# Top-k attention feeding a SwiGLU block: gate and value products of the first four token blocks by halves, and another order of the small units

## The chip, the cores and the metric

The kernel runs on one core of one Trainium2 chip. The metric is the time of one execution on the device in microseconds; lower is better. A profile of one execution stands beside the times.

## What is computed

For 8 batches of 8 heads, with 576 tokens and 64 dimensions a head, scores are q·k divided by 8. Each row keeps its scores down to the 32nd largest; the others become -1e9, and a softmax over the row weighs the values. The heads' results side by side give 4608 tokens of 512 numbers, which pass a SwiGLU block:

```python
scores = scale * np.matmul(q, k.transpose(0, 1, 3, 2))
kth = np.partition(scores, -top_k, axis=-1)[..., -top_k:-top_k + 1]
scores = np.where(scores >= kth, scores, -1000000000.0)
...
x = np.ascontiguousarray(attn_out.transpose(0, 2, 1, 3)).reshape(B * S, H * D)
g = x @ w_gate
silu = g * (1.0 / (1.0 + np.exp(-g)))
return (silu * (x @ w_val) @ w_out).astype(np.float32)
```

w_gate and w_val are 512 x 1536, w_out is 1536 x 512. All is float32.

## The kernel before, in words

**Attention units.** The work of attention is cut into 160 units (`units`). A whole unit is 128 queries of a pair of heads; a batch has 4 such query tiles for each of its 4 pairs. The 64 queries that are left in a batch make a small unit for each pair, in which both heads share the 128 partitions: it has half the work on DVE. A unit passes these steps, each a function: `scores` (PE matmuls L341, for a small unit L327, ACT copies to `sc`), `select` (DVE: four rounds of MAX8 L362, with three rounds of MATCH_REPLACE8 L366 between them, then L372, which writes the penalty into `e`), `penalize` (POOL: L382 and L384, `e` += `sc`), `weigh` (ACT: exp L393), `normalize` (DVE reciprocal L405, ACT L408), `turn` (PE transposes L420, ACT copies L421) and `values` (PE L440 and L449, ACT copy L460 into `xT`).

**FFN blocks.** `xT[kb]` holds a block of 256 tokens (BLK), all 4 pairs of heads; there are 18 blocks, and `done[kb]` counts the columns that have been written. `feed(kb)` is a generator of a block's FFN work: for each of 6 steps s a gate product and a value product, each 8 matmuls of 256 moving columns (L499) into one tile of a PSUM pool with three buffers (`ps_f`). After a product, ACT works on the tile (for the gate L524 to L526, for the value L531) and POOL multiplies (L527, L532). Then comes the product with `w_out`: block 0 has 24 matmuls of 512 columns (L545, `plain`), every other block seven quarters of 6 matmuls (L585) with sums on POOL (L592, L600, L605, L633 and L571).

**Weights.** The generator `weights` brings the three matrices in 36 pieces and rounds them in three steps: a DMA into `w` (three buffers), three ACT instructions (L116, L118, L119), then a DVE shift (L123) and two POOL instructions (L124, L125). The numbers in `lags` say how many half steps after its start a piece takes its last, second and first step. `ready[0]` counts finished pieces. `need(n)` pushes the generator on until n pieces are ready.

**Order.** Nothing is left to a scheduler: at the end, each engine's instructions are tied to the order in which the program issued them. The main loop goes over n. In round n it issues `penalize(n-1)`, `turn(n-3)`, `values(n-4)`, `scores(n+1)`, `weigh(n-1)`, `select(n)` and `normalize(n-2)`, and in between calls `pieces(k)`, which issues up to k pieces of FFN work, and `rounding(1)` (five times in a round with a whole unit). A piece is 4 matmuls of a product, or 3 of a quarter. `credit` limits the pieces: `share(n)` adds 6.4 or 7 for a whole unit, less what the attention of that round takes on PE, and at most one more than that is kept from round to round. `piece` starts a new block when the block before it is finished and `done` says that all 256 columns are there; else it returns 0. It also flushes the queues `on_act` and `on_pool`, in which the ACT and POOL work on products waits, when two are in them. After the last round, all that is left of the FFN work is issued.

**Small units.** Even batches have their small units last, odd ones first. The loop after `units` mixes, for each even batch, its 4 small units, those of the next batch and the first 4 whole units of the next batch: two small ones, a whole one, and so on.

Of the kernel before, what the change touches and what calls it, by code (L numbers as in the profile page):

```python
# [8 lines left out]
AF = mybir.ActivationFunctionType  # L9
ALU = mybir.AluOpType  # L10
FP32 = mybir.dt.float32
# [4 lines left out]
P = 128  # L16
# [4 lines left out]
BLK = 256  # L21
# [4 lines left out]
def kernel(  # L26
# [39 lines left out]
    nc = tc.nc  # L66
    B, H, S, D = q.shape
    DM, DFF = w_gate.shape
    J = S // P
    JP = J * P  # L70
    R = S - JP
    NHP = H // 2
    KC = DM // P
    MC = DFF // P
    MS = MC // 2
    MQ = MC // 2
    NBLK = B * S // BLK
    scale = 1.0 / float(D) ** 0.5
# [8 lines left out]
    ffn = ctx.enter_context(tc.tile_pool(name="ffn", bufs=2))  # L87
# [13 lines left out]
    wg = consts.tile([P, KC, DFF], FP32, name="wg")  # L101
    wv = consts.tile([P, KC, DFF], FP32, name="wv")
# [24 lines left out]
    def weights():  # L127


        pieces = []  # L130
        for f in range(0, DFF, WP):
            for src, dst in ((w_gate, wg), (w_val, wv)):
                for c in range(0, KC, 2):
                    rows = src[c * P : (c + 2) * P, f : f + WP]
                    pieces.append((
                        rows.rearrange("(c p) f -> p c f", p=P), dst[:, c : c + 2, f : f + WP]
                    ))
        for c in range(MC):
            pieces.append((
                w_out[c * P : (c + 1) * P].rearrange("p (c f) -> p c f", c=2),  # L140
                wo[:, c].rearrange("p (c f) -> p c f", c=2),
            ))
        pieces = [rounded(*p) for p in pieces]
        step = [0] * len(pieces)

        def upto(i, k):

            while 0 <= i < len(pieces) and step[i] < k:
                next(pieces[i], None)
                step[i] += 1  # L150


        lags = (3, 2, 0)
        for n in range(2 * len(pieces) + 4):
            for k, lag in enumerate(lags):
                if (n - lag) % 2 == 0:
                    upto((n - lag) // 2, len(lags) - k)
            ready[0] = max((n - 5) // 2 + 1, 0)
            early[0] = lambda: upto(n // 2, 2)
            yield  # L160
        early[0] = lambda: None


        add, sub = ALU.add, ALU.subtract
        lo, hi = slice(0, DM // 2), slice(DM // 2, DM)
        room = []
        for _ in range(3):
            t = ffn.tile([P, 4, DM // 2], FP32, tag="w", name="t", bufs=3)
            room += [t[:, 0:2], t[:, 2:4]]
        for m in range(0, MQ, 2):  # L170
            mm, nn = slice(m, m + 2), slice(MQ + m, MQ + m + 2)
            t3 = room.pop()
            nc.gpsimd.tensor_tensor(t3, wo[:, nn, hi], wo[:, mm, hi], sub)
            T[7] += [t3[:, i, :] for i in range(2)]
            yield
        while not plain_done:
            yield
        for m in range(0, MQ, 2):
            mm, nn = slice(m, m + 2), slice(MQ + m, MQ + m + 2)
            t1 = wo[:, mm, hi]  # L180
            nc.gpsimd.tensor_tensor(t1, t1, wo[:, mm, lo], sub)
            T[5] += [wo[:, m + i, hi] for i in range(2)]
            yield
            t2 = room.pop()
            nc.gpsimd.tensor_tensor(t2, wo[:, nn, hi], t1, sub)
            T[6] += [t2[:, i, :] for i in range(2)]
            yield
            t4 = conv.tile([P, 2, DM // 2], FP32, tag="size", name="t4", bufs=3)
            nc.gpsimd.tensor_tensor(t4[:], wo[:, nn, lo], t2, sub)
            T[4] += [t4[:, i, :] for i in range(2)]  # L190
            yield
        T[1] += [wo[:, m, lo] for m in range(MQ)]
        T[2] += [wo[:, MQ + m, lo] for m in range(MQ)]
        T[3] += [wo[:, MQ + m, hi] for m in range(MQ)]
        yield
# [5 lines left out]
    weight = weights()  # L201
# [2 lines left out]
        for _ in range(n):  # L204
            next(weight, None)

    def need(n):

        while ready[0] < n:
            next(weight)  # L210

    pairs = [(b, hp) for b in range(B) for hp in range(NHP)]
    raw, preps = {}, {}
# [62 lines left out]
    def column(b, qt):  # L276

        return b * S + (qt * P if b % 2 == 0 else 0 if qt == J else R + qt * P)
# [1 line left out]
    units = [(b, qt, hp) for b in range(B) for qt in tiles(b) for hp in range(NHP)]  # L280


    for b in range(0, B - 1, 2):
        n0 = (b * (J + 1) + J) * NHP
        mixed = units[n0 : n0 + 3 * NHP]
        small_ends, small_begins, whole = (
            mixed[i * NHP : (i + 1) * NHP] for i in range(3)
        )
        small_ones = [
            small_ends[0], small_ends[1], small_ends[2], small_begins[0],  # L290
            small_ends[3], small_begins[1], small_begins[2], small_begins[3],
        ]
        units[n0 : n0 + 3 * NHP] = [
            x for i in range(NHP) for x in (*small_ones[2 * i : 2 * i + 2], whole[i])
        ]
    same_pair = {}
    for n, (b, _, hp) in enumerate(units):
        same_pair.setdefault((b, hp), []).append(n)
# [182 lines left out]
    def flush(queue):  # L481
        while queue:
            queue.pop(0)()

    def feed(kb):

        x = xT.pop(kb)  # L490
        hs = []

        def product(w, s, then):
            ps = ps_f.tile([P, 2, BLK], FP32, tag="f", name="f")
            need(4 * s + (2 if w is wg else 4))
            for i in range(2):
                m = 2 * s + i
                for kc in range(KC):
                    nc.tensor.matmul(  # L499
                        ps[:, i, :],  # L500
                        w[:, kc, m * P : (m + 1) * P],
                        x[:, kc, :],
                        start=(kc == 0),
                        stop=(kc == KC - 1),
                    )
                if i == 1:
                    on_act.append(lambda: then(ps))
                yield 1

        plain = kb == 0  # L510
        first, late = slice(0, P), slice(P, BLK)
# [2 lines left out]
            "p (m t) -> p m t", t=P  # L514
        )

        for s in range(MS):
            h = ffn.tile([P, 2, BLK], FP32, tag="h", name="h", bufs=MS + 1)
            hs.append(h)


            def gate(ps, h=h):
                half = ffn.tile([P, 2, BLK], FP32, tag="gv", name="half_g", bufs=3)
                nc.scalar.activation(h[:], ps[:], AF.Tanh, scale=0.5)  # L524
                nc.scalar.mul(half[:], ps[:], 0.5)
                nc.scalar.add(h[:], h[:], 1.0)  # L526
                on_pool.append(lambda: nc.gpsimd.tensor_mul(h[:], h[:], half[:]))  # L527

            def value(ps, h=h, s=s):
                val = ffn.tile([P, 2, BLK], FP32, tag="gv", name="val", bufs=3)  # L530
                nc.scalar.copy(val[:], ps[:])  # L531
                on_pool.append(lambda: nc.gpsimd.tensor_mul(h[:], h[:], val[:]))  # L532

            yield from product(wg, s, gate)
            yield from product(wv, s, value)
        o = ffn.tile([P, 2, DM], FP32, tag="o", name="o", bufs=1)
        if plain:
            for t in range(2):
                ps = ps_f.tile([P, DM], FP32, tag="f", name="o_ps")
                for m in range(MC):  # L540
                    need(4 * MS + m + 1)
                    if m == 6:
                        flush(on_act)
                        flush(on_pool)
                    nc.tensor.matmul(  # L545
                        ps[:],
                        hs[m // 2][:, m % 2, t * P : (t + 1) * P],
                        wo[:, m, :],
                        start=(m == 0),
                        stop=(m == MC - 1),  # L550
                    )
                    if m == MC - 1:

                        def finish(ps=ps, t=t):
                            nc.scalar.copy(o[:, t, :], ps[:])
                            store(o[:, t, :], kb * BLK + t * P)

                        on_act.append(finish)
                        if t == 1:
                            plain_done.append(True)  # L560
                    if m % 2 == 1:
                        yield 1
            return
# [123 lines left out]
    current = []  # L687

    def piece():

        if len(on_act) > 1:
            flush(on_act)
        if len(on_pool) > 1:
            flush(on_pool)
        while True:
            if not current:
                if not todo or done.get(todo[0], 0) < NHP * BLK:
                    return 0
                flush(on_act)
                flush(on_pool)  # L700
                current.append(feed(todo.pop(0)))
            cost = next(current[0], 0)
            if cost == 0:
                current.pop()
                continue
            return cost

    def fetch(n):

# [18 lines left out]
        return beside * n_heads(units[n][1]) / 2 - others  # L728

    def pieces(n):  # L730
        for _ in range(n):
            if credit[0] >= 1:
                credit[0] -= piece()

    def run(steps):
        for _ in steps:
# [128 lines left out]
```

## Time and profile before

| | us |
|---|---|
| median of 8 runs (1825.26 to 1828.7) | 1825.59 |
| the profiled execution | 1827.02 |
| its span, first to last instruction | 1825.2 |
| PE busy / weight loads | 1701.4 / 1404.4 |
| DVE busy | 1612.9 |
| ACT busy | 1218.1 |
| POOL busy | 1040.7 |

The profile comes from the hardware's profiler. "Busy" is the time in which an engine had at least one instruction; PE's matmuls overlap, so their mean duration (383 ns for 256 columns) is longer than the distance between them. A float32 matmul leaves two records in the trace, a transpose one. "Granted clock" is the share of PE's full clock. The slices of the profile cut the span into 40 parts of 45.6 us, each with a digit for tenths of busy time. In a list by time, each line merges instructions of one group: start, duration, group and count, and in brackets the idle time before it and what ended it.

### The profile page before, as it was taken

The page shows a single profiled execution, that of the slowest core. Times are in us where ns is not written, and L with a number is a line of the kernel's source. Part 1 is how long each engine was busy: PE and PEld are TensorE (multiplying, and loading weights), DVE is VectorE, ACT ScalarE, POOL GpSimd, SP SyncE. Part 2 cuts the span into 40 slices and gives each one's busy share as a digit, 9 for nine tenths or more (in the row PEclk, how much of TensorE's full clock was granted, in tenths as well). Part 3 has the DMA queues.
Part 4 walks back from the last instruction along what each step waited for, and adds up shares of the span by engine and source line. Part 5 has one row for each costly group of instructions (what it writes and reads, how often), then busy time and mean ns, then how long its engine had stood idle before and what let it go on. Part 6 is the DMA issues. An engine that isn't in the chain of part 4 may idle for free.

```text
span 1825.2 us, 30457 instructions
## 1 busy us (share of the span) xinstructions
PE 1701.4 (93%) x10756; PEld 1404.4 (77%) x10756; DVE 1612.9 (88%) x3372; ACT 1218.1 (67%) x2945; POOL 1040.7 (57%) x930
## 2 busy tenths in 40 slices
PE   3458999999999999799999999999999999999999
PEld 2346767788888877688888867788888878788888
DVE  7999999999999898999999988999999989998500
ACT  6788767676767576667767676667776767575532
POOL 5878654656464645466565635474556554555544
PEclk6768999999999999899999999999999999999999
DMA  7433011001200011001200011000200011000000
GB/s 195 130 95 103 15 40 42 14 1 39 52 13 1 13 42 41 14 1 31 60 13 1 12 43 41 15 8 7 71 19 7 7 23 40 7 12 1 13 12 12
DMA packets 109033, 59.65 MB, mean 33 GB/s; under 512 B 88272, under 2 KB 96720, under 8 KB 108880
## 3 DMA queue, kind: packets, MB, share of 16 engines
q1 hardware_dynamic: 107680, 57.30, 11.7%
q8 instruction: 85, 1.39, 0.3%
q14 instruction: 68, 0.56, 0.1%
q10 hardware_dynamic: 1200, 0.39, 0.1%
HBM read 48.23 MB, written 9.44 MB: 32 GB/s over the span
## 4 chain that ended last, share of the span: by engine, by line
PE 84%; DVE 6%; ACT 5%; POOL 3%; issue 2%; DMA 0%; SPq 0%; POOLq 0%; DVEq 0%; ACTq 0%
PE f L499 42%; PE x_ps L585 8%; PE av L449 8%; PE etps L420 8%; PE s L341 7%; PE y_ps L585 6%; DVE m L362 2%; DVE rest L366 2%; PE s L327 1%; PE av L440 1%; ACT e L393 1%; PE o_ps L545 1%; PE kqps L265 1%; POOL e L384 1%; ACT e L408 1%
## 5 line engine op out<-in xcount | busy, mean ns | idle before, releaser
L362 DVE MAX8 m<-rest 128x8 f32<-128x576 f32 x864 | 616.7, 753 | 2.2
L366 DVE MATCH_REPLACE8 rest<-m,rest 128x576 f32<-128x576 f32 x576 | 425.7, 749 | 0.0
L384 POOL TENSOR_TENSOR e<-e,sc 128x1152 f32<-128x1152 f32 (+1 forms) x160 | 383.0, 2394 | 71.6 <-DVE e L372 59.4
L499 PE MATMUL f<-xT,wg 128*128 128x256 f32 x1728 | 402.9, 383 | 0.0
L499 PE MATMUL f<-xT,wv 128*128 128x256 f32 x1728 | 399.8, 382 | 0.0
L499 PEld LDWEIGHTS f<-xT,wg 128*128 128x128 f32 x1728 | 322.7, 190 | 65.4 <-issue 23.5
L499 PEld LDWEIGHTS f<-xT,wv 128*128 128x128 f32 x1728 | 323.9, 190 | 58.5 <-issue 16.2
L527 POOL TENSOR_TENSOR h<-h,half_g 128x512 f32<-128x512 f32 x108 | 139.8, 1294 | 338.4 <-ACT h L526 331.9
L421 ACT COPY et<-etps 128x512 f32<-128x512 f32 (+2 forms) x448 | 184.3, 484 | 156.8 <-PE etps L420 155.8
L362 DVE MAX8 m<-sc 128x8 f32<-128x576 f32 x288 | 205.9, 753 | 85.4 <-ACT sc L346 50.5
L420 PE MATMUL etps<-ident,e 128*128 128x128 f32 (+1 forms) x1312 | 185.2, 285 | 98.3 <-issue 37.0
L393 ACT ACTIVATE e<-e,bias 128x576 f32<-128x576 f32 x288 | 221.7, 774 | 80.7 <-POOL e L384 80.6
L420 PEld LDWEIGHTS etps<-ident,e 128*128 128x128 f32 (+1 forms) x1312 | 158.1, 146 | 128.5 <-issue 45.3
L532 POOL TENSOR_TENSOR h<-h,val 128x512 f32<-128x512 f32 x108 | 142.0, 1315 | 163.2 <-ACT val L531 163.0
L408 ACT ACTIVATE e<-e,tot 128x576 f32<-128x576 f32 x288 | 211.7, 790 | 1.9 <-DVE tot L405 1.8
L366 DVE MATCH_REPLACE8 rest<-m,sc 128x576 f32<-128x576 f32 x288 | 212.5, 747 | 0.0
L372 DVE TENSOR_SCALAR e<-sc,m 128x576 f32<-128x576 f32 x288 | 184.2, 680 | 3.4
L341 PE MATMUL s<-kqT 64*128 64x288 f32 x1024 | 171.3, 451 | 8.9 <-ACT kqT L270 8.9
L449 PE MATMUL av<-et,v 128*64 128x128 f32 (+1 forms) x2560 | 170.1, 278 | 0.0
L346 ACT COPY sc<-s 128x288 f32<-128x288 f32 x512 | 164.5, 403 | 3.1 <-PE s L341 3.1
L449 PEld LDWEIGHTS av<-et,v 128*64 128x64 f32 x2560 | 133.7, 142 | 22.6 <-issue 5.9
L524 ACT ACTIVATE h<-f 128x512 f32<-128x512 f32 x108 | 65.3, 605 | 127.6 <-PE f L499 127.6
(73 smaller groups left out, 2028.9 us busy)
## 6 DMA issues: line engine op xcount, KB each, us to landing
v<-in_v_dram SPq DMA_DIRECT2D x32, 256.0 KB, 2.9
kq_in<-in_k_dram SPq DMA_DIRECT2D x63, 128.0 KB, 2.9
kq_in<-in_q_dram SPq DMA_DIRECT2D x63, 128.0 KB, 2.9
out_dram<-o SPq DMA_DIRECT2D x31, 256.0 KB, 2.4
w<-in_moe_w_gate_dram SPq DMA_DIRECT2D x12, 512.0 KB, 3.7
w<-in_moe_w_val_dram SPq DMA_DIRECT2D x12, 512.0 KB, 3.8
w<-in_moe_w_out_dram SPq DMA_DIRECT2D x12, 512.0 KB, 3.6
out_dram<-o SPq DMA_DIRECT2D x9, 128.0 KB, 2.3
```

Of the source, the lines that this page charges most:

```text
L341: nc.tensor.matmul(ps[:, 0:half], slab[d, q0 : q0 + P], slab[d, k0 : k0 + half])
L362: nc.vector.max(m[:, t, 8 * r : 8 * r + 8], cur[:, hs])
L366: nc.vector.match_replace(rest[:, hs], m[:, t, 8 * r : 8 * r + 8], cur[:, hs], LOWEST)
L372: nc.vector.tensor_scalar(e[:, hs], sc[:, hs], m[:, t, TOP_K - 1 : TOP_K], FAR, ALU.is_lt, ALU.mult)
L384: nc.gpsimd.tensor_tensor(e[:, every], e[:, every], sc[:, every], ALU.add)
L393: nc.scalar.activation(e[:, hs], e[:, hs], AF.Exp, bias=bias[:, t : t + 1], scale=scale, accum_out=tot[:, t : t + 1],)
L408: nc.scalar.mul(e[:, hs], e[:, hs], tot[:, t : t + 1])
L420: nc.tensor.transpose(ps[0:kl, c * P : (c + 1) * P], e[:, k0 : k0 + kl], ident[:])
L421: nc.scalar.copy(et[0:kl, c0 : c0 + cn, :], ps[0:kl, 0 : cn * P].rearrange("p (c j) -> p c j", c=cn),)
L449: nc.tensor.matmul(av[hh * R : (hh + 1) * R, 0:ql], v_last[:, hh, :] if c == J else vt[:, hh, c, :], moving, start=last and c == 0, stop=c ...
L499: nc.tensor.matmul(ps[:, i, :], w[:, kc, m * P : (m + 1) * P], x[:, kc, :], start=(kc == 0), stop=(kc == KC - 1),)
L585: nc.tensor.matmul(ps, lhsT, T[i][m], start=m == 0, stop=m == MQ - 1)
```

## The change

Blocks 0 to 3 (`kb < 4`) run their gate and value products over 128 columns at a time: first all 12 products for columns 0 to 127, then all 12 for columns 128 to 255. Each product of a half takes a `ps_f` tile of its own, and ACT and POOL work on half as many elements twice as often. The first half may start when the first 128 columns of the block are done. A piece of a half product counts 0.5 in `credit` and in `pieces`. A product whose weights are not ready no longer pushes the rounding on (`need`) but yields 0 (`until`), which `pieces` takes as nothing to do. The third step of a weight piece comes one piece later (`lags`). The small units of batches 0 and 1 are no longer mixed, so they are 8 units in a row; those of batches 2 and 3 and of 6 and 7 are mixed with the last whole units of the first of the two batches (LAST), those of 4 and 5 with the first whole units of the second (NEXT), as before.

```diff
-        lags = (3, 2, 0)
+        lags = (5, 2, 0)
...
-    def need(n):
+    def until(n):
 
         while ready[0] < n:
-            next(weight)
+            yield 0
...
-    for b in range(0, B - 1, 2):
-        n0 = (b * (J + 1) + J) * NHP
-        mixed = units[n0 : n0 + 3 * NHP]
...
+    NEXT, LAST = "a0 a1 B0 a2 b0 B1 a3 b1 B2 b2 b3 B3", "A0 A1 a0 a1 A2 b0 a2 b1 A3 a3 b2 b3"
+    for b in range(2, B - 1, 2):
+        mix = LAST if column(b, J) % BLK else NEXT
+        tile_of = dict(a=(b, J), b=(b + 1, J), A=(b, J - 1), B=(b + 1, 0))
+        mixed = [(*tile_of[x[0]], int(x[1])) for x in mix.split()]
+        n0 = min(units.index(u) for u in mixed)
+        units[n0 : n0 + len(mixed)] = mixed
...
+    def parts(kb):
+
+        return [slice(0, P), slice(P, BLK)] if kb < 4 else [slice(0, BLK)]
...
-        def product(w, s, then):
+        def product(w, s, c, then):
+            n = c.stop - c.start
+            yield from until(4 * s + (2 if w is wg else 4))
             ps = ps_f.tile([P, 2, BLK], FP32, tag="f", name="f")
-            need(4 * s + (2 if w is wg else 4))
             for i in range(2):
                 m = 2 * s + i
                 for kc in range(KC):
                     nc.tensor.matmul(
-                        ps[:, i, :],
+                        ps[:, i, 0:n],
                         w[:, kc, m * P : (m + 1) * P],
-                        x[:, kc, :],
+                        x[:, kc, c],
...
                 if i == 1:
-                    on_act.append(lambda: then(ps))
-                yield 1
+                    on_act.append(lambda: then(ps[:, :, 0:n], c))
+                yield n / BLK
...
+        for c in parts(kb):
+            while done[kb] < NHP * c.stop:
+                yield 0
+            for s in range(MS):
+                if c.start == 0:
+                    hs.append(ffn.tile([P, 2, BLK], FP32, tag="h", name="h", bufs=MS + 1))
+                h = hs[s]
...
+                def gate(ps, c, h=h):
+                    half = ffn.tile([P, 2, BLK], FP32, tag="gv", name="half_g", bufs=3)
+                    hc, gc = h[:, :, c], half[:, :, c]
+                    nc.scalar.activation(hc, ps, AF.Tanh, scale=0.5)
+                    nc.scalar.mul(gc, ps, 0.5)
+                    nc.scalar.add(hc, hc, 1.0)
+                    on_pool.append(lambda: nc.gpsimd.tensor_mul(hc, hc, gc))
...
+                yield from product(wg, s, c, gate)
+                yield from product(wv, s, c, value)
...
-                if not todo or done.get(todo[0], 0) < NHP * BLK:
+                if not todo or done.get(todo[0], 0) < NHP * parts(todo[0])[0].stop:
                     return 0
...
-            cost = next(current[0], 0)
-            if cost == 0:
-                current.pop()
-                continue
-            return cost
+            cost = next(current[0], None)
+            if cost is not None:
+                return cost
+            current.pop()
...
     def pieces(n):
-        for _ in range(n):
-            if credit[0] >= 1:
-                credit[0] -= piece()
+        while n > 0 and credit[0] >= 1:
+            size = piece()
+            if not size:
+                break
+            credit[0] -= size
+            n -= 0.5 if size == 0.5 else 1
```

More of the change, by code (lines that the diff above doesn't have):

```diff
@@ L280 @@
     units = [(b, qt, hp) for b in range(B) for qt in tiles(b) for hp in range(NHP)]
-    for b in range(0, B - 1, 2):
-        n0 = (b * (J + 1) + J) * NHP
-        mixed = units[n0 : n0 + 3 * NHP]
[L286 to L295, printed above, removed]
+    NEXT, LAST = "a0 a1 B0 a2 b0 B1 a3 b1 B2 b2 b3 B3", "A0 A1 a0 a1 A2 b0 a2 b1 A3 a3 b2 b3"
[5 more added lines that the diff above has]
+        units[n0 : n0 + len(mixed)] = mixed
     same_pair = {}
@@ L483, in flush @@
             queue.pop(0)()
+    def parts(kb):
+        return [slice(0, P), slice(P, BLK)] if kb < 4 else [slice(0, BLK)]
     def feed(kb):
-        x = xT.pop(kb)
+        x = xT[kb]
         hs = []
-        def product(w, s, then):
+        def product(w, s, c, then):
+            n = c.stop - c.start
+            yield from until(4 * s + (2 if w is wg else 4))
             ps = ps_f.tile([P, 2, BLK], FP32, tag="f", name="f")
-            need(4 * s + (2 if w is wg else 4))
             for i in range(2):
@@ L515, in feed, with value @@
         )
[L517 to L535, printed above, removed]
+        for c in parts(kb):
[12 more added lines that the diff above has]
+                    on_pool.append(lambda: nc.gpsimd.tensor_mul(hc, hc, gc))
+                def value(ps, c, h=h):
+                    val = ffn.tile([P, 2, BLK], FP32, tag="gv", name="val", bufs=3)
+                    hc, vc = h[:, :, c], val[:, :, c]
+                    nc.scalar.copy(vc, ps)
+                    on_pool.append(lambda: nc.gpsimd.tensor_mul(hc, hc, vc))
+                yield from product(wg, s, c, gate)
+                yield from product(wv, s, c, value)
+        del xT[kb]
         o = ffn.tile([P, 2, DM], FP32, tag="o", name="o", bufs=1)
@@ L540, in feed @@
                 for m in range(MC):
-                    need(4 * MS + m + 1)
+                    yield from until(4 * MS + m + 1)
                     if m == 6:
```

## The prediction

> **What bounds the kernel now.** I read the 40 slices first, then the engines' busy time in stretches, then the order of time on PE and DVE, and last the two kernels' instruction lists, engine by engine.
>
> ```profile
> PE   3458999999999999799999999999999999999999
> ...
> DVE  7999999999999898999999988999999989998500
> ...
> PEclk6768999999999999899999999999999999999999
> ```
>
> PE is idle for a large part of the first three slices and of slice 17; from slice 4 on it is full. DVE is full from the start, and ends about two and a half slices before PE. So there are two bounds: DVE at first, PE later, and a tail in which PE works alone on FFN blocks.
>
> ```profile
> 101.70:151.40 49.70, 24.03 (x144) 19.44 (x142) 48.04 (x103) 40.19 (x90) 38.32 (x29) 0.64 0.36 106
> 151.40:203.60 52.20, 52.15 (x312) 43.46 (x310) 49.27 (x99) 44.96 (x101) 46.84 (x35) 1.00 0.19 59
> ...
> 1698.60:1825.20 126.60, 123.06 (x648) 107.34 (x646) 16.93 (x30) 45.38 (x95) 59.64 (x61) 1.00 0.03 9
> ```
>
> The columns are PE, PEld, DVE, ACT, POOL, then clock. I call "slot n" the stretch on PE from the score matmuls of unit n (the list's 0th, 1st, ...) to those of unit n+1. The first row is slots 8 to 11: no FFN, PE half idle at a granted clock of 0.64, DVE 97% busy. The second is slots 12 to 15: the first FFN matmuls are in them, and PE is full. The last is what follows the last slot's start: FFN alone.
>
> ```profile
> 112.07 1.91 PE L341 MATMUL s<-kqT 64*128 64x288 f32 x8
> 122.25 2.15 PE L420 MATMUL etps<-ident,e 128*128 128x128 f32 x9 [8.28 <-POOL wg L125]
> ...
> 489.48 3.72 PE L499 MATMUL f<-xT,wg 128*128 128x256 f32 x16
> 493.03 3.62 PE L499 MATMUL f<-xT,wv 128*128 128x256 f32 x16
> 496.49 1.89 PE L499 MATMUL f<-xT,wg 128*128 128x256 f32 x8
> 498.21 1.15 PE L420 MATMUL etps<-ident,e 128*128 128x128 f32 x9
> 499.19 0.39 PE L440 MATMUL av<-et,vlast 128*128 128x128 f32 x2
> ```
>
> Above, in slot 9, PE waits 8.28 us between the scores and the next transposes. Below, in slot 44, nothing waits: 16 records (8 matmuls; each is two records) take 3.45 us from start to start, 0.216 each. I call 4 matmuls of 256 columns, 1.73 us, a piece. A whole unit's attention takes PE 3.5 us at full clock (9 transposes 0.98, values 1.35, scores 1.17). Summing each slot's matmuls with these durations gives the measured slot within 0.1 us in most slots from 32 on: PE sets the time there. The sum over all slots is 1636 us of PE work; the rest of the 1825.2 us is waits and half clock.
>
> ```profile
> 732.77 1.42 DVE L362 MAX8 m<-sc 128x8 f32<-128x576 f32 x2
> ...
> 743.32 1.43 DVE L362 MAX8 m<-sc 128x8 f32<-128x576 f32 x2
> ```
>
> One whole unit takes DVE 10.55 us (start to start), a small one half of it. With the usual 4 to 5 pieces a slot's PE work is 10.4 to 12.2 us, so PE is ahead of DVE as the bound. FFN work is free only where it is missing now: in the early slots and the starved ones.
>
> **Part 1: half blocks, earlier start.** By the instruction lists block 0's first half may start after 4 units instead of 8. Pieces issued, summed up to and with each slot:
>
> slot 11: 0 before, 12 after; slot 18: 29, 41.5; slot 24: 47, 51.5; slot 31: 70.5, 82.5; slot 47: 138.8, 139.5; slot 70: 208.5, 221.5; slot 145: 498.5, 504.5; slot 158: 558.5, 570.5; end: 622.5 both.
>
> The lead of 12 pieces comes from slots 8 to 10 (5.5, 5, 1.5). It is lost at slots 45 to 47 (2.25, 0 and 0 pieces: block 4 isn't ready) and won back when the kernel before starves at slots 69 and 70 (0 and 0). What is left behind the last slot falls from 64 pieces to 52. PE work is only moved, so I sum idle time instead. Slots 8 to 11 last 49.7 us with 14.0 us of attention at full clock: 35.7 lost. After, they hold 14.0 + 12 x 1.77 = 35.3 of work (1.77 is a piece of 16 half records); if they still last 49.7, 14.4 is lost: **-21.3 us**.
>
> Do they still last 49.7? PE's wait of 8.28 us is cover: slot 8's 5.5 pieces end at about 113 us, and scores 9 reach DVE some 7 us before it wants them. ACT and POOL get 11 half products in two slots, beside 5 weight pieces. POOL's pieces of work: e-add 2.64, weight piece 2.7, half product about 0.75 (the 128x256 rows L592 and L600 take 0.74 to 0.78). Slot 8: 3.1 + 3 x 2.7 + 4 x 0.75 = 14.2; slot 9: 12.3; then 12.7 and 9.3: 48.5 in all, just under 49.7. Slots 12 to 15 of before held a like mix in 52.2. So the bounds are 0 and +2.5: I take **+1.5**. Some products of slot 9 wait in PE's queue for POOL's rounding of their weights; behind them are the transposes and scores 10, for which the same 7 us are cover.
>
> **Part 2: 128 columns instead of 256.** Four blocks: 4 x 384 records of 128 columns for 4 x 192 of 256, with twice the weight loads. The trace has no such product. Near rows: the 9 transposes with 9 loads above take 0.98 us, 0.109 each, half of 0.216; the two records of L440 lie 0.111 apart, and with the drain after them 0.16. At 0.109 to 0.1105 the four blocks cost +1 to +3.5; at 0.16 each, about +66. I take **+2**, because the transposes are a stream with a load for each record, as this is.
>
> [...]
>
> A product now fills one of three PSUM tiles in 1.75 us instead of 3.46, so the fourth product waits for ACT 5.2 us after the first began. At 546.3 us the scores end, ACT's score copies end at 548.6 and its first gate could follow at once: free by about 549.6, against 551.6. Nothing waits there. Where POOL's e-add is late, ACT's exp waits (16.0 us in 7 waits before 152 us, the longest 3.2) and the spare is gone. Two half instructions also cost ACT and POOL more than a whole one: by ACT's 0.50 us for 512 elements and 0.32 for 288 about 0.09 each, on POOL 2 x 0.75 against 1.29; for a block some 2.2 and 2.5 us, beside PE's 42. Blocks 1 to 3 have their half products in about 16 slots; 1.5 us in each would be +24, none 0; I take **+3**, nearer to the slot above, where ACT has 2 us to spare.
>
> **Part 3: the order of small units.** Batch 0's small units now come eight in a row, not mixed. Slots 16 to 31 hold 137.3 us of PE work before and lasted 148.4: 11.1 lost. After, 138.7 us of work; the eight small slots hold 5.8 to 7.0 us each against DVE's 5.28. Small slots before lost 0.3 (5.45 us slots at 244.6 and 662.5 us) to 1.9 us (around 1080 us). So 2.4 to 15 lost, plus 2.7 in slot 31, still short of pieces: 5 to 18 against 11.1, that is -6 to +7. I take **0**. The orders around batches 2 and 6 change too; batch 4's doesn't. PE work and DVE work by slot are alike there (126.6 against 128.2 us in slots 53 to 67): 0, within 3.
>
> **Part 4: starved slots.** Slots 68 to 71 lasted 40.8 us with 25.8 of PE work: 15.0 lost. After, slots 45 to 48 hold 26.7; DVE's four units set 40.8 again: 14.1. I take 0.
>
> **Part 5: weight rounding.** The third step of a weight piece comes one piece later. DVE's shift waited for ACT 7 times, 6.7 us in all, before 152 us, in the DVE-bound stage; these waits should go. The buffer's next DMA then waits longer, and ACT's next weight step may wait for it, ahead of an exp and score copies: some 3.7 us to land. Between -6.7 and +2: **-1**.
>
> **Sum:** -21.3 + 1.5 + 2 + 3 + 0 + 0 - 1 = -15.8 us. The profiled execution took 1827.02 us (span 1825.2), 1.4 over the median of 1825.59; so 1811.2 for it, and **1810 us** as median.
>
> **Rivals.** (a) *Given back*: the half products wait for ACT and PSUM, or the eight small units in a row wait for the chain DVE, POOL, ACT. For it: three PSUM tiles, POOL near full early. Against: 5.45 us small slots exist. +8 to +15 on the sum: 1818 to 1825. (b) *Slower*: a 128-column record isn't 0.109 us because its own weight load shows. Place: blocks 0 (second half) to 3 on PE's full stretch, 1344 records. It decides from (15.8 + 2) / 1344 = 0.013 us over 0.108, so from 0.121. [...] (c) *More*: DVE's waits and the small units both improve: -6 each: 1798 to 1801. (d) *The lead isn't there*, FFN still starting when it did because weights or credit hold it: 1825. The instruction list speaks against it.
>
> **How the numbers follow.** Forecast (1801 to 1818): 0.70; (a) 0.14, about half of it below 1822; (b) 0.06; (c) 0.08; (d) 0.02. 0.2% of the median, 3.65 us, is about what a measurement of this kernel can tell from no change. Faster: 0.70 + 0.08 + 0.07 = 0.85; same 0.08; slower 0.07. The range 1800 to 1821 takes in the forecast, part of (c) and half of (a).
>
> **What would show it.** FFN matmuls from about 103 us, PE busy over 35 us in 101 to 152; 128-wide records 0.109 us apart; scores of unit 12 still near 151 us; the starved place near slot 46, at about 500 us; behind the last scores some 106 us instead of 126.6. Wrong, if PE shows idle time before L499 for ACT, if slots 8 to 11 take over 55 us, or if the small run loses over 2 us in each slot.

## The result and the profile after

The changed kernel takes **1835.66 us** (median of 10 runs, 1833.62 to 1838.41), against 1826.86 for the kernel before (28 runs, 1824.9 to 1828.7): a ratio of 1.005, 95% interval 1.0041 to 1.0058. The forecast was 1810, faster; it is slower by some 9 us. The profiled execution's span is 1833.8 us, 8.6 more than before. In the code after, the rows of before have other line numbers: scores L336 and L322, transposes L415, values L435 and L444, gate on ACT L529 to L531, value on ACT L537, POOL's products L532 and L538, the penalty's addition on POOL L379, exp L388, normalize L403, score copies L341 and L327, copies of the transposes L416; L499 and the rounding's L116 to L125 keep theirs.

The slices of the changed kernel:

```profile
PE   4577899999989999999999999999999998999999
...
DVE  7999779999999899999999989999999988999700
...
PEclk9788899999989999999999999999999999999999
```

PE is fuller in the first three slices, the third above all (7 after 5), but not in the fourth (7 after 8). And DVE, full there before, has a 7 in the fifth and the sixth slice (183 to 275 us). The sixth holds the small units of batches 0 and 1, where PE is full; in the fifth, which slots 12 to 15 take up for the most part, PE isn't full either. The stretches of slots 8 to 11, slots 12 to 15 and the tail, with the columns as before:

```profile
98.90:158.70 59.80, 43.28 (x334) 37.91 (x332) 55.27 (x108) 49.37 (x120) 48.44 (x41) 0.87 0.31 96
158.70:224.50 65.80, 57.46 (x370) 43.54 (x368) 56.63 (x112) 42.86 (x107) 49.70 (x43) 0.91 0.16 53
...
1725.10:1833.80 108.70, 102.99 (x552) 89.00 (x550) 12.74 (x28) 39.30 (x83) 51.57 (x55) 0.99 0.03 10
```

The tail is 18.0 us shorter, nearly what was meant. Ahead of it all is given back: slots 8 to 11 take 59.8 us instead of 49.7, slots 12 to 15 take 65.8 instead of 52.2. In the second row DVE is busy for 56.6 of 65.8 us and PE for 57.5: neither is full, so something else lies on the path.

The same for the whole kernel, by slots. "Lost" is the slot time less its PE work at full clock:

| stretch | before, us / lost | after, us / lost |
|---|---|---|
| slots 0–7 | 93.8 / 71.1 | 91.0 / 68.4 |
| slots 8–11 | 49.7 / 35.7 | 59.8 / 24.6 |
| slots 12–15 | 52.2 / 1.8 | 65.8 / 15.1 |
| slots 16–31 | 148.4 / 11.1 | 150.1 / 11.4 |
| slots 44–48 | 56.8 / 0.3 | 50.8 / 14.2 |
| slots 68–72 | 53.1 / 15.1 | 57.3 / 0.3 |
| slots 96–111 | 153.6 / 14.4 | 146.1 / 8.2 |
| slots 134–149 | 145.1 / 8.4 | 156.3 / 18.0 |
| tail | 126.7 | 108.7 |

The stretches left out differ by at most 1.5 us in what they lose. In duration it adds up to -2.8 (0–7), +10.1, +13.6, +1.7 (16–31), -5.5 (32–133), +9.4 (134 to the last scores), -18.0: +8.5. Two places stand out: slots 8 to 15, which lose 39.7 us where 17.7 were forecast (14.4 + 1.5 + 1.8), and slots 134 to 149, which lose 9.6 more than before where 0 was forecast.

**Slots 8 to 15.** PE in slots 8 and 9 of the changed kernel, by time:

```profile
103.86 1.95 PE L499 MATMUL f<-xT,wv 128*128 128x128 f32 x16
105.65 1.95 PE L499 MATMUL f<-xT,wg 128*128 128x128 f32 x16
107.43 1.95 PE L499 MATMUL f<-xT,wv 128*128 128x128 f32 x16
...
122.44 1.95 PE L499 MATMUL f<-xT,wv 128*128 128x128 f32 x16
130.63 2.05 PE L499 MATMUL f<-xT,wg 128*128 128x128 f32 x8 [6.24 <-ACT val L537]
132.47 2.13 PE L415 MATMUL etps<-ident,e 128*128 128x128 f32 x9
```

The first three rows start 1.785 us apart, 0.1116 for a record. Then PE stands for 6.24 us, with the next transposes queued behind the product: all three PSUM tiles hold products that ACT hasn't read. ACT in that time:

```profile
122.74 1.47 ACT L403 ACTIVATE e<-e,tot 128x576 f32<-128x576 f32 x2
128.46 0.66 ACT L116 ACTIVATE size<-w 128x512 f32<-128x512 f32 x1 [4.25 <-DMA w<-in_moe_w_val_dram]
129.03 0.66 ACT L118 ACTIVATE w<-w 128x512 int32<-128x512 uint32 x1
129.59 0.65 ACT L119 ACTIVATE w<-w 128x512 f32<-128x512 f32 x1
130.14 0.35 ACT L537 COPY val<-f 128x256 f32<-128x256 f32 x1
```

ACT has the value's copy to do, and it would free the tile. Ahead of it in ACT's queue stands the first step of a weight piece, whose DMA hasn't landed. POOL shows why that DMA came late:

```profile
123.34 1.39 POOL L125 TENSOR_TENSOR wg<-size,w 128x512 f32<-128x512 f32 x1
```

L125 is a piece's third step and the last reader of its `w` buffer. It ends at 124.73; the next DMA into that buffer is issued at 124.75, and ACT starts on what it brought at 128.46, 3.7 us later. With the old lag this third step was issued one piece earlier. The waits between 98 and 226 us, with total, number and longest in us:

```profile
DVE size L123 <- ACT size L116: 13.7, 3, 4.7
...
PE f L499 <- ACT val L537: 12.3, 2, 6.2
ACT size L116 <- DMA w<-in_moe_w_out_dram: 11.4, 3, 6.2
...
ACT size L116 <- DMA w<-in_moe_w_val_dram: 7.2, 2, 4.2
```

ACT stands for weights 18.6 us in 5 waits, and PE and DVE stand behind it. The first of the five, 2.96 us, ends at 98.32 and so just ahead of slot 8; three that end at 128.46, 186.50 and 208.35 hold 14.7 us. The slots hit are 9, 13 and 15 (21.58, 21.50 and 16.90 us, against 14.60, 12.40 and 12.68 before).

**Slots 134 to 149**, around batch 6's small units. PE and ACT in slot 139:

```profile
1500.61 1.52 PE L322 MATMUL s<-kqT 64*64 64x288 f32 x7
1502.07 3.72 PE L499 MATMUL f<-xT,wv 128*128 128x256 f32 x16
1507.18 1.38 PE L415 MATMUL etps<-ident,e 128*128 128x128 f32 x9 [1.40 <-issue]
```

```profile
1502.08 0.68 ACT L327 COPY sc<-s 128x288 f32<-128x288 f32 x2
1505.82 0.58 ACT L537 COPY val<-f 128x512 f32<-128x512 f32 x1 [3.06 <-PE f L499]
1506.31 1.44 ACT L403 ACTIVATE e<-e,tot 128x576 f32<-128x576 f32 x2
```

The slot holds exactly one whole product. ACT is idle for 3.06 us until that ends, because its copy is next in the queue; the normalize behind the copy, which the next transposes need, waits with it. So PE waits after its own product, and DVE then 2.08 us for the scores that follow:

```profile
1511.78 1.42 DVE L357 MAX8 m<-sc 128x8 f32<-128x576 f32 x2 [2.08 <-ACT sc L341]
```

Slots 138 to 144 lose 3.32, 2.64, 2.65, 0.01, 0.69, 3.16 and 1.65 us. Slots 139, 140 and 142 to 144 hold one whole product each. Slot 138 holds only half a product; there ACT waits 2.36 us for the end of a quarter (at 1488.45), and POOL's sum of that quarter stands ahead of the penalty's addition, for which the exp waits 1.03 us.

### The profile page after: what moved, and what is told of

Same layout as the page of the kernel before. It is cut to its first block, busy times and chain, and to the rows that moved or that the text cites. A ratio compares the mean times of both kernels' runs of the same rounds, so it can differ in the third digit from the quotient of the medians.

```text
span 1833.8 us, 32186 instructions
## 1 busy us (share of the span) xinstructions
PE 1714.5 (93%) x11524; PEld 1435.6 (78%) x11524; DVE 1613.4 (88%) x3372; ACT 1224.3 (67%) x3041; POOL 1044.1 (57%) x978
## 3 DMA queue, kind: packets, MB, share of 16 engines
q1 hardware_dynamic: 107680, 57.30, 11.5%
## 4 chain that ended last, share of the span: by engine, by line
PE 82%; ACT 7%; DVE 4%; POOL 3%; issue 2%; DMA 1%; SPq 0%; POOLq 0%; ACTq 0%
PE f L499 40%; PE x_ps L592 9%; PE av L444 8%; PE etps L415 8%; PE s L336 7%; PE y_ps L592 6%; DVE m L357 2%; ACT e L388 2%; DVE rest L361 2%; PE s L322 1%; PE av L435 1%; ACT e L403 1%; ACT sc L341 1%; PE kqps L265 1%; PE o_ps L552 1%
## 5 line engine op out<-in xcount | busy, mean ns | idle before, releaser
L499 PE MATMUL f<-xT,wg 128*128 128x256 f32 (+1 forms) x2112 | 410.9, 345 | 12.3 <-ACT val L537 12.3
L499 PE MATMUL f<-xT,wv 128*128 128x256 f32 (+1 forms) x2112 | 408.5, 344 | 2.2 <-POOL wv L125 1.8
L379 POOL TENSOR_TENSOR e<-e,sc 128x1152 f32<-128x1152 f32 (+1 forms) x160 | 383.0, 2394 | 44.4 <-DVE e L367 34.2
L499 PEld LDWEIGHTS f<-xT,wg 128*128 128x128 f32 x2112 | 342.8, 192 | 67.3 <-issue 28.6
L499 PEld LDWEIGHTS f<-xT,wv 128*128 128x128 f32 x2112 | 342.5, 191 | 55.7 <-issue 20.3
L532 POOL TENSOR_TENSOR h<-h,half_g 128x512 f32<-128x512 f32 (+1 forms) x132 | 143.6, 1088 | 322.0 <-ACT h L531 320.0
L416 ACT COPY et<-etps 128x512 f32<-128x512 f32 (+2 forms) x448 | 184.6, 484 | 155.6 <-PE etps L415 154.7
L538 POOL TENSOR_TENSOR h<-h,val 128x512 f32<-128x512 f32 (+1 forms) x132 | 144.3, 1093 | 212.5 <-ACT val L537 211.0
L388 ACT ACTIVATE e<-e,bias 128x576 f32<-128x576 f32 x288 | 221.8, 775 | 58.8 <-POOL e L379 58.5
L415 PE MATMUL etps<-ident,e 128*128 128x128 f32 (+1 forms) x1312 | 185.4, 285 | 75.1 <-ACT e L403 25.5
L415 PEld LDWEIGHTS etps<-ident,e 128*128 128x128 f32 (+1 forms) x1312 | 157.0, 146 | 103.3 <-ACT e L403 35.2
L403 ACT ACTIVATE e<-e,tot 128x576 f32<-128x576 f32 x288 | 212.1, 792 | 0.0
L336 PE MATMUL s<-kqT 64*128 64x288 f32 x1024 | 173.7, 449 | 13.9 <-ACT kqT L270 7.5
L367 DVE TENSOR_SCALAR e<-sc,m 128x576 f32<-128x576 f32 x288 | 177.4, 656 | 3.4
L444 PE MATMUL av<-et,v 128*64 128x128 f32 (+1 forms) x2560 | 169.7, 277 | 0.0
L341 ACT COPY sc<-s 128x288 f32<-128x288 f32 x512 | 163.9, 402 | 3.4 <-PE s L336 3.4
L529 ACT ACTIVATE h<-f 128x512 f32<-128x512 f32 (+1 forms) x132 | 69.9, 529 | 129.1 <-PE f L499 128.9
L444 PEld LDWEIGHTS av<-et,v 128*64 128x64 f32 x2560 | 133.6, 142 | 22.6 <-issue 6.1
```

What stands on the lines that cost most here:

```text
L336: nc.tensor.matmul(ps[:, 0:half], slab[d, q0 : q0 + P], slab[d, k0 : k0 + half])
L341: nc.scalar.copy(sc[:, i * half : (i + 1) * half], ps[:, 0:half])
L379: nc.gpsimd.tensor_tensor(e[:, every], e[:, every], sc[:, every], ALU.add)
L388: nc.scalar.activation(e[:, hs], e[:, hs], AF.Exp, bias=bias[:, t : t + 1], scale=scale, accum_out=tot[:, t : t + 1],)
L403: nc.scalar.mul(e[:, hs], e[:, hs], tot[:, t : t + 1])
L415: nc.tensor.transpose(ps[0:kl, c * P : (c + 1) * P], e[:, k0 : k0 + kl], ident[:])
```

## The experiments

**Theory A**: slots 8 to 15 are late because a piece's third step comes one piece later, so that ACT waits for weight DMAs. **Rival B**: they are late because the half products load ACT, POOL and the three PSUM tiles in slots that had no room; the lag only shows where. For slots 134 to 149, one theory is that the new order of batch 6's small units costs it, the other that it is the **phase**: which half of a product falls into which short slot.

**e1_lag3**, the changed kernel with the old lag:

```diff
-        lags = (5, 2, 0)
+        lags = (3, 2, 0)
```

> The changed kernel with the rounding's lags back at (3, 2, 0); all else as changed. Theory A (the stagger): slots 8 to 15 lost some 23 us because the third step of a weight piece comes one piece later, so its buffer is free later, the next piece's DMA starts later, and ACT's next weight step waits for that DMA at the head of its queue, with PE (products waiting for PSUM) and DVE (the shift) behind it. Then this kernel gets back most of it: 1814 to 1820 us against 1835.7, slots 8 to 15 last 101 to 108 us instead of 125.6, and ACT's waits for the weight DMA in that stage are gone. Theory B (the load): half products and rounding together are too much for POOL, ACT and three PSUM tiles, whatever the lag: 1833 to 1838 us, with PE's waits before the half products still there.

1826.35 us against 1825.4 beside it: 1.0005 (0.9996 to 1.0015). Slots 8 to 15 lose 28.2 us instead of 39.7; ACT has no wait for a weight DMA there any more. So A holds for 11.5 us and not for the rest. What is left there, 98 to 216 us:

```profile
DVE size L123 <- ACT size L116: 14.5, 6, 3.9
ACT e L388 <- POOL e L379: 12.5, 5, 5.1
...
PE f L499 <- ACT val L537: 8.2, 4, 2.6
```

DVE waits for ACT, ACT for POOL, PE for ACT, with no DMA in it: three engines in a ring, each well filled (in slots 8 to 11 of e1, 56.6 us, DVE is busy for 50.4, ACT for 47.5, POOL for 48.1).

**e3_before_lag5**, the kernel before with the new lag, `lags = (5, 2, 0)`:

> The kernel before with only the lags of the changed one, (5, 2, 0). Theory A: the later third step alone makes ACT wait for weight DMAs wherever POOL is late; before, FFN products meet the rounding only in slots 12 to 15, so a part of the loss should show there: +3 to +12 us, 1829 to 1838. If the stagger hurts only together with the early half products, the change of time is -3 to +1 us, as the first slots become some 2.8 us shorter: 1823 to 1827.

1825.02 us, 0.9993 (0.9984 to 1.0002). Slots 0 to 7 lose 3.6 us less, slots 12 to 15 lose 4.2 more, slots 16 to 31 lose 1.8 less. By itself the lag is no loss: it becomes one where products stand in ACT's queue behind the weight step, which before is the case from slot 12 on only.

**e4_next**, the changed kernel with the order NEXT for all three pairs of batches:

```diff
-        mix = LAST if column(b, J) % BLK else NEXT
+        mix = NEXT
```

> The changed kernel, but batches 2 and 6 mixed in the pattern NEXT, as the kernel before had them, instead of LAST (batches 0 and 1 stay unmixed). Theory C: the order LAST costs the some 9 us that slots 134 to 150 lost in the changed kernel: 1825 to 1829 us. Theory D: these were lost to the position of the FFN blocks against the small units, which the lead shifts by 12 pieces, and the order matters little: 1834 to 1838 us.

1846.78 us, 1.0115 (1.01 to 1.013). I had taken the order for a matter of batch 6; neither theory gave this. PE starves at slots 46 and 47, as in the changed kernel, and then again in slots 68 to 72 (14.9 us lost there, against 0.3); the tail is 126.9 us again with 64 pieces: the lead of 12 pieces is gone. LAST for batches 2 and 3 is what keeps it. Slots 134 to 149 lose 9.9.

**e5_before_new_order**, the kernel before with the new loop over `units` alone:

> The kernel before with only the new order of units (batches 0 and 1 unmixed, 2 and 6 in LAST). Theory C: slower by 6 to 10 us: 1832 to 1836. Theory D: within 3 us of before, 1823 to 1829. The eight small units in a row cost nothing in the changed kernel's profile (11.4 us lost in slots 16 to 31, against 11.1), so both theories take 0 for them.

1829.0 us, 1.0016 (1.0007 to 1.0026). The order wins the tail alone (110.7 us, 53 pieces, as slots 68 to 72 no longer starve), and slots 134 to 149 lose 6.9 us, less than before. So LAST doesn't cost anything at that place as such. But slots 53 to 67 lose 22.4 instead of 8.6. Part of that is lost in slots 55 and 56, which hold no product. Still, slots 59, 60 and 62 to 64 hold one whole product each and lose some 11 us, where they lose some 2 in the changed kernel with the same order of units: there slots 63 and 64, for instance, have the second half of one product and the first half of the next. That speaks for the phase.

**f3_phase** tests it: e1 with one piece, half a product, less of credit in round 136 (slot 137 holds 5 pieces instead of 6), so that the products behind it lie half a product later against the slots:

```diff
+        if n == 136:
+            credit[0] -= 1.0
```

> As e1_lag3, with one piece of credit taken away in round 136, so that from slot 138 on the FFN pieces stand half a product later against the units; the order of units stays. Theory H (phase): a small slot with one whole product waits for the product's end, ACT's gate or copy, the normalize behind it in ACT's queue and then the transposes; if the slot holds the second half of one product and the first half of the next, ACT gets its work earlier. Then slots 134 to 149 lose 8 to 12 us instead of 19.7: 1814 to 1819 us. If the order LAST or the lead costs the time, the loss stays at 18 to 20 and the time at 1825 to 1828.

**1817.59 us**, 0.9948 (0.9932 to 0.9965), faster than both kernels. Slots 134 to 149 lose 5.9 us, against 19.7 in e1, with the same order and, in slots 138 to 145, the same number of pieces in each slot. PE, two slots of it (one of unit 139, the other of unit 140):

```profile
1489.16 1.99 PE L499 MATMUL f<-xT,wg 128*128 128x256 f32 x8
1491.00 1.89 PE L499 MATMUL f<-xT,wv 128*128 128x256 f32 x8
1493.56 1.38 PE L415 MATMUL etps<-ident,e 128*128 128x128 f32 x9 [0.67 <-issue]
...
1496.92 1.99 PE L499 MATMUL f<-xT,wv 128*128 128x256 f32 x8
1498.75 1.89 PE L499 MATMUL f<-xT,wg 128*128 128x256 f32 x8
1500.48 0.71 PE L415 MATMUL etps<-ident,e 128*128 128x128 f32 x5
```

```profile
1491.20 0.60 ACT L529 ACTIVATE h<-f 128x512 f32<-128x512 f32 x1 [0.51 <-PE f L499]
...
1498.95 0.59 ACT L537 COPY val<-f 128x512 f32<-128x512 f32 x1 [0.59 <-PE f L499]
1499.43 0.78 ACT L403 ACTIVATE e<-e,tot 128x576 f32<-128x576 f32 x1
```

Each slot now holds the second half of one product and the first half of the next. ACT gets its product 2.0 us after the scores (1489.16 to 1491.20) and not 3.75 (1502.07 to 1505.82 in the changed kernel), waits 0.5 to 0.6 us, and the normalize behind it is done while PE is on the other half.

**h1_after_phase**, the changed kernel, its lag kept, with that line only:

> The changed kernel itself (lags 5, 2, 0) with only the piece of credit taken away in round 136, as in f3_phase. If the phase of the products against the small units and the lags are two causes that add, the phase alone gives back the 9 us that it gave on top of the lags: 1825 to 1828 us, with 5 to 8 us lost in slots 134 to 149 and 38 to 41 in slots 8 to 15. If it gives back less than 4 us here, the two are not independent.

1824.99 us, 0.9993 (0.9984 to 1.0003): 10.7 us under the changed kernel. Slots 134 to 149 lose 5.9, slots 8 to 15 still 39.9. The two causes are separate. Together with the old lag (f3) it is 7.4 us less again.

Three tries were meant to mend the rest of slots 8 to 15. **f1_shared_psum** is e1 with gate and value of a half product in the two halves of one `ps_f` tile:

```diff
-            ps = ps_f.tile([P, 2, BLK], FP32, tag="f", name="f")
+            if not box:
+                box.append(ps_f.tile([P, 2, BLK], FP32, tag="f", name="f"))
+            ps = box[0]
+            at = 0 if w is wg or n == BLK else n
...
-                        ps[:, i, 0:n],
+                        ps[:, i, at : at + n],
...
```

> As e1_lag3 (lags 3, 2, 0), and the gate and the value product of a half share one PSUM tile, 128 columns each, so that six half products fit in three tiles instead of three. e1_lag3 lost 28.2 us of PE time in slots 8 to 15, where 17.7 were forecast. Theory P (PSUM): PE waits there for ACT to empty a tile (8.2 us in 4 waits) and that delays the rest; then the loss falls to 18 to 22 us and the time to 1816 to 1821. Theory L (load of ACT and POOL): the order of ACT's and POOL's work stays, so the loss stays at 25 to 29 us and the time at 1824 to 1828, with the waits moved elsewhere.

1840.87 us, 1.0081 (1.0066 to 1.0096), a miss with the opposite sign. The wait moved and grew (98 to 216 us; this run's L502 and L533 are L499 and L530 of the changed kernel):

```profile
PE f L502 <- ACT half_g L533: 14.0, 5, 4.8
```

The value product now waits for ACT's readers of the gate, which has the same tile. Slots 8 to 15 lose 32.5 us, slots 16 to 31 lose 22.9 instead of 11.9. That PSUM buffers are the lack isn't shown by this, nor refuted: the edit gave fewer of them in effect.

**f2_spread** is e1 with the products of slots 8 to 11 spread three pieces to a slot:

```diff
+        if 7 <= n < 11:
+            credit[0] = min(credit[0], 3.5)
```

> As e1_lag3, and the credit is cut to 3.5 in rounds 7 to 10, so that the first half block's 12 pieces lie 3, 3, 3, 3 in slots 8 to 11 instead of 5.5, 5, 1.5, 0; the amount of work and all later slots stay nearly the same. Theory L: it is the burst in two slots beside five weight pieces that ACT and POOL can't follow; the loss in slots 8 to 11 falls from 21.4 to 14 to 17 us: 1819 to 1823 us in all. If load is not the matter, these slots lose 20 us or more again: 1825 to 1828.

1829.31 us, 1.0016 (1.0007 to 1.0026). Slots 8 to 15 lose 25.1 instead of 28.2 (slots 8 to 11 some 20, against 21.4), slots 16 to 31 lose 15.5 instead of 11.9. So for the most part the loss isn't from the burst of 5 pieces in slots 8 and 9.

**f4_all** is f1, f2 and f3 together, with the new lag up to the 36th half step of the rounding and the old one from there:

> The shared PSUM tiles, the spread of the first 12 pieces and the later phase in one kernel, with the lags at 5 for the first 36 half steps (to about slot 7) and at 3 from then on. If the four effects add: 2.8 us in the first slots, 6 to 12 in slots 8 to 15 and 8 to 10 in slots 134 to 149, all against e1_lag3: 1802 to 1810 us. If the phase and the load theory both fall: 1822 to 1826.

1829.66 us, 1.0014 (1.0005 to 1.0024): they don't add up. Slots 16 to 31 lose 23.3 us, as with f1. **g1_lag_switch** is f3 with only that switch of the lag:

```diff
+            lags = (5, 2, 0) if n < 36 else (3, 2, 0)
+            if n == 36:
+                upto(16, 3)
```

> As f3_phase, with the lags at 5 for the first 36 half steps (to about slot 7) and at 3 from then on. The later third step shortened slots 0 to 7 by 2.7 to 3.6 us in the changed kernel and in e3_before_lag5, as DVE's shift no longer waits for ACT; its cost came in slots 9, 13 and 15. If both hold, 1813 to 1816 us, with 67 to 68.5 us lost in slots 0 to 7 and 25 to 29 in slots 8 to 15. If the gain of the first slots only moves the same wait to slots 8 to 11: 1816 to 1819.

1817.29 us, 0.9944 (0.9931 to 0.9958), no different from f3. Slots 0 to 7 lose 67.5 instead of 71.3, and the 3.8 us are given back: slots 8 to 15 lose 3.0 more and 16 to 31 lose 1.5 more.

The last two take load away, and so measure what it costs. **g2_no_pool_mult** is f3, in which block 0 leaves out POOL's 24 multiplications (its tokens come out otherwise); **g3_less_act** is f3, in which block 0 leaves out the gate's second and third ACT instruction and POOL's product of the two, 24 ACT and 12 POOL instructions:

> As f3_phase, but block 0 leaves out POOL's 24 multiplications of half gate and value products (17.5 us of POOL work in slots 8 to 16; the first 256 tokens come out otherwise). Theory L1 (POOL): POOL's queue is what delays the e-add, and with it ACT's exp, and the weight pieces; then slots 8 to 15 lose 16 to 21 us instead of 27.1, and the time is 1807 to 1813. If POOL isn't the cause: 25 to 28 lost, 1816 to 1819.

> As f3_phase, but block 0 leaves out the gate's second and third ACT instruction and POOL's product of the two (24 ACT instructions, 6.5 us of ACT's time, and 12 of POOL's 24 multiplications, 8.8 us, in slots 8 to 16; the first 256 tokens come out otherwise). Theory L2 (ACT): ACT, in which gates, weight steps, exp and copies stand in one queue, is what DVE's shift and PE's products wait for; then slots 8 to 15 lose 14 to 20 us, less than in g2, and the time is 1806 to 1812. If ACT isn't the cause, it lies between f3_phase and g2, nearer to half way: 22 to 25 lost.

1809.36 us, 0.9905 (0.9892 to 0.9919), and 1809.5 us, 0.9902 (0.9888 to 0.9915). Slots 8 to 15 lose 21.1 and 19.3 us, against 27.1 in f3: POOL's load and ACT's both count. DVE's wait for the weight step in f3, g2 and g3, 98 to 212 us:

```profile
DVE size L123 <- ACT size L116: 14.9, 6, 3.3
```

```profile
DVE size L123 <- ACT size L116: 13.6, 6, 3.6
```

```profile
DVE size L123 <- ACT size L116: 7.8, 6, 2.4
```

ACT's exp waits less for POOL's addition in both (4.2 and 4.8 us, against 12.1 in f3); DVE's wait for ACT stays nearly as it was without POOL's products, and is halved with less for ACT. By 0.75 us for a half product on POOL and 0.27 on ACT (start to start), g2 takes 18 us from POOL and gains 6.0; g3 takes 9 from POOL and 6.5 from ACT and gains 7.8. If POOL's microsecond is worth the same in both, ACT's is worth about 0.7 and POOL's 0.33; that split is an estimate and no run shows it by itself.

## Why the prediction was wrong

**Part 5, weight rounding, -1: the step that failed most.** It named the right event ("ACT's next weight step may wait for it, ahead of an exp and score copies: some 3.7 us to land") and priced it at one such wait, -6.7 to +2. There were five, 18.6 us on ACT, three of them 4.2 to 6.2 us long, and what stood behind them was not only exp and copies but the readers of PSUM tiles that PE needed. It cost slots 8 to 15 11.5 us (after against e1) to 12.8 (h1 against f3), less 2 to 4 us that slots 0 to 7 gain. DVE's seven waits before 152 us, which "should go", became two (6.7 us before, 4.8 after), but one of these is 4.5 us long, and two more of 4.5 and 4.7 us came later: 13.7 us between 98 and 226. The gain and the loss were weighed in the kernel before, where e3 shows them to balance; the question was what the wait does in the kernel after, together with Part 1.

The ACT rows from 122.74 to 130.14 show ACT keep to the order of its queue: the copy that PE waited for had its product (on PE from 118.87 to 120.82) before PE's wait of 6.24 us began at 124.39, and started only behind the weight step, at 130.14.

**Part 1, "do they still last 49.7?", +1.5.** They lasted 59.8, over the 55 that were named as a sign of being wrong, and with the old lag 56.6 (e1). The sum for POOL was right: 48.5 forecast, 48.44 measured. The conclusion from it was wrong. "Just under" the slot time is enough for one engine with work always at hand; here DVE, POOL and ACT follow each other for each unit, and each is well filled (55.3, 48.4 and 49.4 of 59.8 us). Beside the lag the ACT and POOL work of block 0's half products costs slots 8 to 15 another 6 to 8 us (g2, g3 leave out part of it), with about 1.6 left between g3's 19.3 and the forecast's 17.7. What the half products add to the three PSUM tiles, named in Part 2, isn't separated from that. And filling alone doesn't explain it: in slots 12 to 15 of the kernel before, with whole products, DVE, ACT and POOL are busy for 49.3, 45.0 and 46.8 of 52.2 us, and only 1.8 us are lost. Why that load fits beside whole products and not beside half ones stays open. The early start itself came as forecast: FFN from 101.97 us (103), and a lead of 12 pieces in the tail. The scores of unit 12 stand at 158.7 us instead of the 151 that was to stay.

**Part 2, 128 columns.** The record takes 0.1116 us (103.86 to 107.43, two products), not 0.109: 4 x 384 x 0.1116 is 171.4 us, against 4 x 41.6 in whole products (the last block's 12 take from 1770.12 to 1811.67): +5.0 us (+5.5 by 0.216 a record), where +2 was taken and +3.5 was the bound. The transposes were the right neighbour, a little too cheap. Half of the 0.216 of a 256-column record is 0.108: a record of 128 columns takes 3% more for each column, and is well under the 0.121 from which rival (b) decides. Rival (b) falls.

**Part 3, the order, 0.** Right for slots 16 to 31: 11.4 lost against 11.1, and for slots 53 to 67 (8.8 against 8.6). Wrong for batch 6: "PE work and DVE work by slot are alike there: 0, within 3" holds for the sums and not for where in a slot a product begins. +9.6 us, all of it the phase (f3, h1). Slots 96 to 111 lose 6.2 less than before, also not forecast. The phase could do that too: before, slots 101 and 107 hold one whole product each and lose 1.9 and 3.4 us; after, slot 101 holds quarters alone and slot 107 half a product, and they lose 0.1 and 1.3. No run tried it.

**Part 4, starved slots, 0**: right. They went to slots 44 to 48 and lose 14.2 us there, 14.1 forecast, at 523 to 551 us (500 forecast, as the slots ahead took longer).

**The tail**: -18.0 us and not -20.8. With less FFN work left, PE waits 0.78 and 1.09 us before the last two units' transposes, where it waited for none before; that is 1.9 of the 2.8 us.

**The sum and the rivals.** Forecast -15.8, measured +8.6 in the span. The difference of 24.4 is 22.0 in slots 8 to 15, 9.6 in slots 134 to 149, 3.0 in the 128 columns and 2.8 in the tail, less 1.8 that slots 0 to 7 won beyond Part 5's -1, 6.2 in slots 96 to 111, and the 3 that Part 2 took for blocks 1 to 3 and no stretch shows. That leaves -2.0, spread over stretches that differ by at most 1.5. Rival (a), given back, had a part of what happened at the first place (half products that wait for ACT and PSUM), and stopped at 1825. Its other place, the small units in a row (slots 16 to 31), lost nothing; the loss came in the mixed ones of batch 6. No rival had the weight step at the head of ACT's queue.

## What to carry to other kernels

In the changed kernel a weight step that waited 4.25 us for its DMA held up all that stood behind it in ACT's queue, and PE for 6.24 us: before an instruction that waits for a DMA is moved later or its buffer is freed later, list all that other engines need from behind it, in the kernel as it will be and not as it is. Where several engines that follow each other are each 80 to 95% full (DVE 92, ACT 83 and POOL 81% in slots 8 to 11 of the changed kernel), a sum for each that just fits is no proof of room: an addition can cost a third to a half of its time on the engines, as here (6.0 of 18 us in g2, 7.8 of 15.5 in g3). And where a slot is short, look at which part of a product falls into it: moving the boundary by half a product gained 10.7 us with not one instruction less.

## What the runs showed of the hardware beyond that

In f1, two products that share a PSUM tile aren't two buffers: PE waited for the readers of the other half, 14.0 us in 5 waits. Whether the program's handling of tiles or the chip makes it wait, no run tells. A stream of float32 matmuls of 128 columns, each record with its own weight load (16 loads from 103.75 us on beside the 16 records from 103.86 on, in the changed kernel), runs at 0.1116 us a record, 3% more per column than one of 256 at 0.216.

What stays open: the last 1.6 us of slots 8 to 15, the split of the load between ACT, POOL and PSUM there, and the gain in slots 96 to 111. The best kernels are f3 and g1, 0.9948 and 0.9944 of the kernel before; what the early start and the order are worth, with the phase set right, is thus some 9 to 10 us, of the 15.8 that were forecast.
